# A DiT block on one core: batch 1's input from a second queue, one more matmul row before two scale groups, and a gate vector folded by copies

## The chip, the cores and the metric

The kernel runs on one NeuronCore of a Trainium2 chip. Its engines are TensorE (matrix multiplication), VectorE (elementwise work and reductions), ScalarE (activation functions, also elementwise), GpSimd and SyncE; the last issues most of the DMAs here. In the profile they are PE (with PEld for TensorE's weight loads), DVE, ACT, POOL and SP. The metric is the device time in microseconds of one execution; lower is better.

## What is computed

A transformer block with adaptive layer norm. Two batches of 256 tokens of width 1152, two heads of 576, and a hidden width of 4608, in bf16:

```python
B, N, D = (2, 256, 1152); F = 4 * D; H = 2
mod = (_silu(c) @ w_mod).reshape(B, 6, 1, D)
shift_a, scale_a, gate_a, shift_m, scale_m, gate_m = [mod[:, i] for i in range(6)]
h = _layernorm(x, axis=-1) * (1 + scale_a) + shift_a
qkv = (h @ wqkv).reshape(B, N, 3, H, Dh)
# ... softmax attention of q, k, v over each batch and head ...
x = x + gate_a * (a @ wo)
h2 = _layernorm(x, axis=-1) * (1 + scale_m) + shift_m
m = _gelu(h2 @ w_fc1) @ w_fc2
return x + gate_m * m
```

The six modulation vectors come from the small input c (two rows of 1152) and a matrix of 1152 x 6912. Two of them matter below: scale_a, which is needed at the very start, and gate_m, which is needed at the very end.

## The kernel before: the parts that are touched

The weights stream through a ring of large buffers, nearly all of them issued in order from SyncE's queue (`nc.sync`). The kernel begins with x, whose 512 rows are four tiles of 128 partitions. A partition of a batch holds two neighbouring rows of x, one in each of the batch's two tiles, so that tiles 0 and 1 are batch 0 and tiles 2 and 3 batch 1.

```python
    x_v = x.rearrange("b (p l) d -> p b l d", l=TPB)
# ...
    x_sb = act.tile([P, NT, D], BF16, name="x_sb", tag="x_sb")
    c_sb = act.tile([B * KD, P], BF16, name="c_sb")
    nc.scalar.dma_start(c_sb[:], c_v)
    touch_x = act.tile([P, 32], BF16, name="touch_x")
    nc.scalar.dma_start(touch_x[:], x_v[:, 1, 0, 0:32])
    for t in (0, 1, 3, 2):
        nc.sync.dma_start(x_sb[:, t, :], x_v[:, t // TPB, t % TPB, :])
```

After x come the scale weights in groups of columns, each followed by the rows of the K weights that it is used with:

```python
    SGROUPS = [(0, 2), (2, 4), (4, 6), (6, 8), (8, 9)]
    KM1 = 6
    w_scale_a = wide_tile("w_scale_a")
# ...
    def load_k(k0, k1, c0, c1):
        nc.sync.dma_start(w_k[:, k0:k1, c0:c1], wqkv_v[:, k0:k1, D + c0:D + c1])

    for k0, k1 in SGROUPS:
        nc.sync.dma_start(
            w_scale_a[:, :, k0 * P:k1 * P],
            wmod_v[:, :, S_SCALE_A * D + k0 * P:S_SCALE_A * D + k1 * P],
        )
        for a, z in [(0, 1), (1, 2)] if k0 == 0 else [(k0, k1)]:
            load_k(a, z, 0, KM1 * P)
    load_k(0, KD, KM1 * P, D)
```

A little later in program order ScalarE loads its function tables (`InstLoadActFuncSet`). The layer norm's statistics are split over two engines: ScalarE sums tiles 0 and 2 (`act_stats`), VectorE takes tiles 1 and 3 (`stats_piece`). The normalized tiles are transposed on TensorE, scaled by 1 + scale_a while they are copied out of PSUM (`modulate`, batch 0 on VectorE, batch 1 on ScalarE), and multiplied with the K weights. Instructions of one engine run in the order in which they stand here:

```python
    warm(7, pwarm)
    act_stats(0)
    for j in range(NPD):
        stats_piece(1, j)
    act_mean_eps(0)
    act_root(0)
    nc.scalar.activation(rstd1[:, 1:2], mv1[:, 1, 1:2], ACT.Ln, bias=eps_t[:], scale=1.0)
    root_exp(0, 2)
    act_stats(2)
    for j in range(NPD):
        stats_piece(3, j)
    pool_eps(3)
    pool_rsqrt(3, 4)
    norm1(1, 0, CUT)
    norm1(0, 0, CUT)
    pt_a = transpose_x([0, 1, 2, 3], BT[0])
    act_mean_eps(2)
    act_root(2)
    root_exp(2, 3)
    norm1(3, 0, CUT)
    pm0, pm1 = [scale_group(k, k + 1, acc_tile) for k in range(2)]
    nc.vector.tensor_scalar_mul(hT0[:, 0, 0:N], pt_a[:, 0, :], pm0[:, 0, 0:1])
    nc.vector.tensor_copy(scale_a[:, 0:1, :], pm0[:])
    scale_add(pm1, 1, 2)
    modulate(pt_a, 1, 1, 0, 0, "d")
    norm1(2, 0, N)
    norm1(2, N, CUT)
    pt_c = aux_tile([P, 4, N], "pt", BF16)
    transpose_x([0, 1, 2, 3], [3], pt_c, 1)
    fill(1)
    k_step(0, 0, N)
    k_step(1, 0, N, 0, 2)
    modulate(pt_c, 0, 0, 1, 0, "a", P, N)
    transpose_x([0, 1], [2], pt_c, 0)
    k_step(1, 0, N, 2)
# ...
    k_step(1, N, T)
    k_step(2, 0, N)
    k_step(2, N, T)
    for k in range(3, KD):
        split = 2 if k in (3, 5) else 0
        k_step(k, 0, T, 0, split)
        if k in (3, 5, 7):
            k1 = min(k + 3, KD)
            scale_add(scale_group(k + 1, k1), k + 1, k1)
        if k < KD - 1:
            both(transpose_x([k + 1], range(NT)), k + 1)
        k_step(k, 0, T, split)
    for m in range(KM1):
        k_evac(m)
```

`k_step(k, c0, c1, m0, m1)` adds the product of one chunk k of 128 inputs to output panels m0 to m1 - 1, in columns c0 to c1 (columns 0 to 255 are batch 0, 256 to 511 batch 1). `scale_group` computes 1 + scale_a for a few chunks by matmuls with two columns. `both` modulates a chunk for both batches.

At the end of the block the last gate, gate_m, is needed as a row of 1152 numbers for each batch, spread over all partitions. VectorE multiplies the gate weights by silu(c) and adds up over the nine chunks, which leaves a sum over 128 partitions to be done:

```python
    fold = const.tile([P, 32], FP32, name="fold")
    nc.vector.tensor_reduce(fold[:], ident[:].rearrange("p (q a) -> p a q", a=32), axis=AX.X, op=ALU.add)
    gates_dram = tc.dram_tile([2, B, D], BF16, name="gates_dram")

    def broadcast_gate(g):
        gate = act.tile([P, B, D], BF16, name="gate", tag="gate")
        for b in range(B):
            nc.gpsimd.dma_start(gate[:, b, :], gates_dram[g, b:b + 1, :].partition_broadcast(P))
        return gate
# ...
    def gate_vector(g, wg):
        part = act.tile([P, B, D], FP32, name="part", tag="x_sb")
        folded = small.tile([P, B, D // 32], FP32, name="folded", tag="folded", bufs=1)
        for k in range(KD):
            for b in range(B):
                if k == 0:
                    nc.vector.tensor_scalar_mul(part[:, b, :], wg[:, k, :], s32[:, k, b:b + 1])
                else:
                    nc.vector.scalar_tensor_tensor(
                        part[:, b, :], wg[:, k, :], s32[:, k, b:b + 1], part[:, b, :],
                        op0=ALU.mult, op1=ALU.add,
                    )
        for b in range(B):
            for c in range(0, D, PW):
                blocks = work.tile([P, PW // 32, 32], FP32, name="tmp", tag="tmp", bufs=3)
                nc.vector.transpose(blocks[:].rearrange("p j r -> p (j r)"), part[:, b, c:c + PW])
                nc.vector.tensor_reduce(
                    folded[:, b, c // 32:(c + PW) // 32], blocks[:], axis=AX.X, op=ALU.add
                )

        return lambda: gate_vector_finish(g, folded)

    def gate_vector_finish(g, folded):
        rows = D // 32
        pg = aux_tile([rows, B, 32], "pg")
        for b in range(B):
            nc.tensor.matmul(pg[:, b, :], folded[:, b, :], fold[:], start=True, stop=True)
        nat = work.tile([rows, B, 32], BF16, name="nat_v", tag="nat_v", bufs=1)
        nc.vector.tensor_copy(nat[:], pg[:])
        for b in range(B):
            nc.gpsimd.dma_start(gates_dram[g, b, :].rearrange("(j r) -> j r", r=32), nat[:, b, :])
        return broadcast_gate(g)
```

TensorE does this last sum, with `fold` (four stacked 32 x 32 identities) as the moving operand, just before the last panel of the first MLP matrix; the result goes to DRAM and comes back as a broadcast:

```python
    gate_m = None
    for m in range(MSPLIT, KF):
        pacc = acc_tile([P, T], "pacc")
        for k in range(KD):
            f1_mm(pacc[:], m, k, 0, T, k == 0)
        nc.scalar.activation(gT[:, m, :], pacc[:], ACT.Gelu_apprx_tanh)
        if m == 22:
            gate_m_finish = gate_vector(1, w_gate_m)
        if m == KF - 2:
            gate_m = gate_m_finish()
        if m == MSPLIT:
            load_f2(0)
        if m > MSPLIT and m % KD == KD - 1:
            load_f2(m // KD)
```

The last matrix multiplies the 36 chunks of the hidden layer, and each finished group of 384 columns is multiplied by gate_m on VectorE:

```python
        pacc = acc_tile([P, cw], "pacc")
        for kk in range(KF):
            j, r = divmod(n * KF + kk, 27)
            nc.tensor.matmul(
                pacc[:], gT[:, kk, t * P:(t + 1) * P],
                w_f2[j][:, r, c0 - n * PW:c0 - n * PW + cw],
                start=(kk == 0), stop=(kk == KF - 1),
            )
        tmp = work.tile([P, cw], FP32, name="tmp", tag="tmp", bufs=3)
        nc.vector.tensor_tensor(tmp[:], pacc[:], gate_m[:, b, c0:c0 + cw], op=ALU.mult)
        o_sb = work.tile([P, cw], BF16, name="o_sb", tag="o_sb", bufs=3)
        (nc.vector if last else nc.gpsimd).tensor_tensor(
            o_sb[:], tmp[:], x1[:, t, c0:c0 + cw], op=ALU.add
        )
        nc.sync.dma_start(out_v[:, b, t % TPB, c0:c0 + cw], o_sb[:])
```

Of the kernel before, what the change touches and what calls it, by code (L numbers as in the profile page):

```python
# [8 lines left out]
FP32 = mybir.dt.float32  # L9
BF16 = mybir.dt.bfloat16  # L10
ACT = mybir.ActivationFunctionType
ALU = mybir.AluOpType
AX = mybir.AxisListType
# [6 lines left out]
def kernel(  # L20
# [11 lines left out]
    nc = tc.nc  # L32
    B, N, D = x.shape
# [3 lines left out]
    P = 128  # L37
    T = B * N
    NT = T // P
    TPB = N // P  # L40
    KD = D // P
    KF = F // P
# [10 lines left out]
    const = ctx.enter_context(tc.tile_pool(name="const", bufs=1))  # L53
    act = ctx.enter_context(tc.tile_pool(name="act", bufs=1))
    wide = ctx.enter_context(tc.tile_pool(name="wide", bufs=5))
    work = ctx.enter_context(tc.tile_pool(name="work", bufs=2))
    small = ctx.enter_context(tc.tile_pool(name="small", bufs=4))
# [5 lines left out]
    def aux_tile(shape, name, dt=FP32):  # L63
        return psum.tile(shape, dt, name=name, tag="aux", bufs=2)


    x_v = x.rearrange("b (p l) d -> p b l d", l=TPB)
# [14 lines left out]
    x_sb = act.tile([P, NT, D], BF16, name="x_sb", tag="x_sb")  # L82
# [1 line left out]
    nc.scalar.dma_start(c_sb[:], c_v)  # L84
    touch_x = act.tile([P, 32], BF16, name="touch_x")
    nc.scalar.dma_start(touch_x[:], x_v[:, 1, 0, 0:32])
    for t in (0, 1, 3, 2):
        nc.sync.dma_start(x_sb[:, t, :], x_v[:, t // TPB, t % TPB, :])  # L88

    zeros = const.tile([P, T], BF16, name="zeros")  # L90
# [39 lines left out]
    for (j0, j1), rows in zip(SHG, QROWS):  # L130
# [25 lines left out]
        act_func_set_id=LN_EXP_TABLES, name=nc.get_next_instruction_name(),  # L156
        engine=mybir.EngineType.Activation,
    ))
    neg_half = const.tile([P, B], FP32, name="neg_half")
    nc.gpsimd.memset(neg_half[:], -0.5)  # L160
    early = small.tile([P, 1], FP32, name="early", tag="early", bufs=1)
# [116 lines left out]
    def k_step(k, c0=0, c1=T, m0=0, m1=KM1):  # L278
        for m in range(m0, m1):
            if k == 0 and c0 == 0:  # L280
                pk[m] = acc_tile([P, T], "pk")
            nc.tensor.matmul(  # L282
                pk[m][:, c0:c1], w_k[:, k, m * P:(m + 1) * P], hT0[:, k, c0:c1],
                start=(k == 0 and c0 == 0), stop=(k == KD - 1), skip_group_check=True,
            )
# [112 lines left out]
    k_step(2, 0, N)  # L398
    k_step(2, N, T)
    for k in range(3, KD):  # L400
        split = 2 if k in (3, 5) else 0
        k_step(k, 0, T, 0, split)
        if k in (3, 5, 7):
            k1 = min(k + 3, KD)
            scale_add(scale_group(k + 1, k1), k + 1, k1)
        if k < KD - 1:
            both(transpose_x([k + 1], range(NT)), k + 1)
        k_step(k, 0, T, split)
    for m in range(KM1):
        k_evac(m)  # L410

# [38 lines left out]

    s32 = const.tile([P, KD, B], FP32, name="s32")
    nc.vector.tensor_copy(s32[:], sT[:, :, 0:B])
    fold = const.tile([P, 32], FP32, name="fold")
    nc.vector.tensor_reduce(fold[:], ident[:].rearrange("p (q a) -> p a q", a=32), axis=AX.X, op=ALU.add)
    gates_dram = tc.dram_tile([2, B, D], BF16, name="gates_dram")

    def broadcast_gate(g):
# [7 lines left out]
# [17 lines that stand above are left out]
                    folded[:, b, c // 32:(c + PW) // 32], blocks[:], axis=AX.X, op=ALU.add  # L482
                )

        return lambda: gate_vector_finish(g, folded)

    def gate_vector_finish(g, folded):
        rows = D // 32
        pg = aux_tile([rows, B, 32], "pg")
        for b in range(B):  # L490
            nc.tensor.matmul(pg[:, b, :], folded[:, b, :], fold[:], start=True, stop=True)
        nat = work.tile([rows, B, 32], BF16, name="nat_v", tag="nat_v", bufs=1)
        nc.vector.tensor_copy(nat[:], pg[:])  # L493
        for b in range(B):
            nc.gpsimd.dma_start(gates_dram[g, b, :].rearrange("(j r) -> j r", r=32), nat[:, b, :])  # L495
        return broadcast_gate(g)

    def gate_natural(g, wg):
# [278 lines left out]
# [4 lines that stand above are left out]
            f1_mm(pacc[:], m, k, 0, T, k == 0)  # L781
        nc.scalar.activation(gT[:, m, :], pacc[:], ACT.Gelu_apprx_tanh)  # L782
        if m == 22:
            gate_m_finish = gate_vector(1, w_gate_m)
        if m == KF - 2:
            gate_m = gate_m_finish()
        if m == MSPLIT:
            load_f2(0)
        if m > MSPLIT and m % KD == KD - 1:
            load_f2(m // KD)  # L790
# [9 lines left out]
    for gi, (n, t, c0, cw) in enumerate(groups):  # L800
        b = t // TPB
# [59 lines left out]
```

## Time and profile before

| what | value |
|---|---|
| time, median of 3 runs | 243.47 us (242.92 to 243.62) |
| span of the profiled execution | 241.3 us |
| TensorE busy | 236.3 us |
| first transposes of x on TensorE | 8.64 us |
| first matmul of the last K panels (L311) | 25.41 us |
| first and last matmul of the first MLP matrix (L750) | 97.31 to 167.87 us |
| end of the last matrix's matmuls (L806) | 238.18 us |

In the profile a line such as `L750` is line 750 of the kernel. The chain that ended last is followed back from the last instruction, at each step to whatever released it. The waits say for which other instruction or DMA an engine stood still. The timeline lists instructions in order of time, with equal ones merged: start, busy time, engine, line, operation, result and inputs, and in brackets the idle time before them. Times are microseconds from the start of the span. The ends of matmuls are modelled, so a single matmul in the list is longer than the step from one to the next.

### The profile page before, as it was taken

Reading aid. Unit: us, or ns where it says so; the run is one execution under the profiler, and the core shown is the slowest. Engines: PE = TensorE matmul, PEld = TensorE weight load, DVE = VectorE, ACT = ScalarE, POOL = GpSimd, SP = SyncE. Lnnn points to the kernel's source line nnn. Section 1 sums busy time; section 2 is a strip of 40 time slices with the busy share of each in tenths; the row PEclk is TensorE's granted clock in tenths of the full one; section 3 lists DMA queues with packets and bytes.
Section 4 is the critical chain, followed back from the end, with each engine's and each line's share of the span. In section 5 each row is a group of like instructions: output and inputs, shape, how many; then the busy total and the mean of one; then the engine's idle time right before and its main releaser. Section 6 shows DMA issues by size and latency. Waiting matters only on the chain.

```text
span 241.3 us, 3993 instructions
## 1 busy us (share of the span) xinstructions
PE 236.3 (98%) x1698; PEld 144.6 (60%) x1698; DVE 91.6 (38%) x194; ACT 60.1 (25%) x122; POOL 28.3 (12%) x47
## 2 busy tenths in 40 slices
PE   8899999999999999999999999999999999999994
PEld 5675444466667566888844444444666656666674
DVE  4842442319325678930002999950000000000001
ACT  6732322307215032770423333222000000000000
POOL 2300000001400324100000000001121111111111
PEclk9999999999999999999999999999999999999999
DMA  6999999998599994739999999999300000000000
GB/s 196 324 317 311 376 367 391 389 393 249 99 315 397 387 311 81 196 62 364 390 392 392 339 326 284 285 326 275 98 16 16 20 16 16 19 18 18 26 25 16
DMA packets 48925, 53.30 MB, mean 221 GB/s; under 512 B 9731, under 2 KB 36619, under 8 KB 48907
## 3 DMA queue, kind: packets, MB, share of 16 engines
q1 hardware_dynamic: 41312, 50.14, 62.6%
q10 hardware_dynamic: 7083, 1.72, 4.9%
q0 software_dynamic: 512, 1.19, 2.2%
q8 instruction: 13, 0.21, 0.4%
q14 instruction: 5, 0.04, 0.1%
HBM read 50.15 MB, written 1.19 MB: 213 GB/s over the span
## 4 chain that ended last, share of the span: by engine, by line
PE 95%; DMA 2%; DVE 1%; SPq 0%; issue 0%; DVEq 0%
PE pacc L806 29%; PE pacc L750 29%; PE pacc L697 7%; PE pacc L603 7%; PE pq L525 7%; PE pk L282 5%; PE pk L311 2%; DMA x_sb<-in_x_dram 2%; PE pa L644 2%; PE ps_s L560 2%; PE pn L420 2%; PE pt L267 1%; PE pm L250 1%; DVE stats L195 1%; PE pg L502 0%; SPq L88 0%
## 5 line engine op out<-in xcount | busy, mean ns | idle before, releaser
L750 PE MATMUL pacc<-hT,w_f 128*128 128x256 bf16 (+1 forms) x432 | 70.5, 326 | 0.0
L806 PE MATMUL pacc<-w_f,gT 128*128 128x384 bf16 (+2 forms) x468 | 70.5, 314 | 0.0
L806 PEld LDWEIGHTS <-gT 128*128 128x128 bf16 x468 | 44.4, 98 | 26.2
L750 PEld LDWEIGHTS <-w_f 128*128 128x128 bf16 x432 | 42.2, 98 | 27.6
L812 DVE TENSOR_TENSOR tmp<-pacc,gate 128x384 f32<-128x384 f32 (+2 forms) x13 | 6.9, 527 | 65.6 <-PE pacc L806 57.3
L782 ACT ACTIVATE gT<-pacc 128x512 bf16<-128x512 f32 x24 | 14.3, 597 | 32.7 <-PE pacc L750 32.7
L473 DVE SCALAR_TENSOR_TENSOR part<-w_gate_m,s,part 128x1152 f32<-128x1152 bf16 x16 | 21.4, 1414 | 0.0
L814 POOL TENSOR_TENSOR o_sb<-tmp,x 128x384 bf16<-128x384 f32 (+1 forms) x12 | 11.6, 971 | 53.9 <-DVE tmp L812 53.9
L697 PE MATMUL pacc<-w_o,big 128*128 128x384 bf16 x108 | 17.9, 326 | 0.0
L525 PE MATMUL pq<-hT,w_q 128*128 128x512 bf16 x81 | 17.8, 379 | 0.0
L603 PE MATMUL pacc<-w_v,hT 128*128 128x384 bf16 x108 | 17.7, 326 | 0.0
L603 PEld LDWEIGHTS <-hT 128*128 128x128 bf16 x108 | 10.5, 98 | 7.1 <-issue 0.3
L697 PEld LDWEIGHTS <-big 128*128 128x128 bf16 x108 | 10.4, 98 | 7.2 <-issue 0.4
L525 PEld LDWEIGHTS <-w_q 128*128 128x128 bf16 x81 | 7.9, 98 | 9.4
L282 PE MATMUL pk<-big,w_k 128*128 128x256 bf16 (+1 forms) x72 | 13.2, 325 | 0.0
L703 POOL TENSOR_TENSOR x<-tmp,x_sb 128x384 f32<-128x384 f32 x8 | 7.3, 911 | 26.3 <-DVE tmp L702 26.3
L471 DVE TENSOR_SCALAR part<-w_gate_m,s 128x1152 f32<-128x1152 bf16 x2 | 1.6, 818 | 22.2 <-DMA w_gate_m<-in_w_mod_dram 22.2
L495 POOL DMA_DIRECT2D gates_dram<-nat_v x2 | 1.1, 534 | 67.7 <-DVE nat_v L493 67.7
L282 PEld LDWEIGHTS <-w_k 128*128 128x128 bf16 x72 | 6.8, 97 | 3.5 <-issue 0.2
L771 ACT ACTIVATE gT<-pacc 128x512 bf16<-128x512 f32 x12 | 6.5, 597 | 9.1 <-PE pacc L750 9.1
L516 POOL DMA_DIRECT2D gates_dram<-nat x4 | 2.4, 596 | 49.8 <-DVE nat L513 48.4
L175 PE MATMUL pwarm<-zeros 128*128 128x256 f32 x18 | 6.7, 540 | 1.2 <-DVE eps_t L95 1.2
(106 smaller groups left out, 164.4 us busy)
## 6 DMA issues: line engine op xcount, KB each, us to landing
w_f<-in_w_fc_dram SPq DMA_DIRECT2D x12, 864.0 KB, 14.2
w_f<-in_w_fc_dram SPq DMA_DIRECT2D x3, 1728.0 KB, 10.1
w_f<-in_w_fc_dram SPq DMA_DIRECT2D x2, 2592.0 KB, 17.2
w_gate_a<-in_w_mod_dram SPq DMA_DIRECT2D x3, 864.0 KB, 14.4
w_v<-in_wqkv_dram SPq DMA_DIRECT2D x3, 864.0 KB, 15.4
w_o<-in_wo_dram SPq DMA_DIRECT2D x3, 864.0 KB, 14.7
w_shift_m<-in_w_mod_dram SPq DMA_DIRECT2D x3, 864.0 KB, 9.5
w_scale_m<-in_w_mod_dram SPq DMA_DIRECT2D x3, 864.0 KB, 15.8
```

The lines of the kernel that those rows point to most:

```text
L175: nc.tensor.matmul(dst[:, 0:T // 2], zeros32[:, 0:P], zeros32, start=True, stop=True)
L282: nc.tensor.matmul(pk[m][:, c0:c1], w_k[:, k, m * P:(m + 1) * P], hT0[:, k, c0:c1], start=(k == 0 and c0 == 0), stop=(k == KD - 1), skip_g ...
L473: nc.vector.scalar_tensor_tensor(part[:, b, :], wg[:, k, :], s32[:, k, b:b + 1], part[:, b, :], op0=ALU.mult, op1=ALU.add,)
L525: nc.tensor.matmul(pq[m][:], w_q[:, k, m * P:(m + 1) * P], hT[:, k, :], start=(k == 0), stop=(k == KD - 1), skip_group_check=True,)
L603: nc.tensor.matmul(pacc[:], hT[:, k, t * P:(t + 1) * P], w_v[:, k, pnl * PW:(pnl + 1) * PW], start=(k == 0), stop=(k == KD - 1),)
L697: nc.tensor.matmul(pacc[:], aT[:, k, t * P:(t + 1) * P], w_o[:, k, c0:c1], start=(k == 0), stop=(k == KD - 1),)
L703: (nc.gpsimd if pool_add else nc.vector).tensor_tensor(x1[:, t, c0:c1], tmp[:], x_sb[:, t, c0:c1], op=ALU.add)
L750: nc.tensor.matmul(dst, w_f1[m // KD][:, k, ml * P:(ml + 1) * P], hT[:, k, c0:c1], start=start, stop=(k == KD - 1), **kw,)
L782: nc.scalar.activation(gT[:, m, :], pacc[:], ACT.Gelu_apprx_tanh)
L806: nc.tensor.matmul(pacc[:], gT[:, kk, t * P:(t + 1) * P], w_f2[j][:, r, c0 - n * PW:c0 - n * PW + cw], start=(kk == 0), stop=(kk == KF - 1),)
L812: nc.vector.tensor_tensor(tmp[:], pacc[:], gate_m[:, b, c0:c0 + cw], op=ALU.mult)
L814: (nc.vector if last else nc.gpsimd).tensor_tensor(o_sb[:], tmp[:], x1[:, t, c0:c0 + cw], op=ALU.add)
```

## The change

Three things are changed.

First, SyncE loads only batch 0's two tiles of x, and then goes on to the scale weights. Batch 1's x comes in one load of 128 partitions with two neighbouring rows each (4608 bytes in one piece instead of two of 2304), issued from ScalarE's queue behind the table load, so that it may travel beside the first scale group.

Second, for chunks k = 3 and 5 three panels of the K product, and not two, stand ahead of the next scale group, so that this group's weights may come later; and for k = 4 and 6 the product is done batch by batch.

Third, the last sum of gate_m leaves TensorE: four copies bring the four groups of 32 partitions side by side in 32 partitions, VectorE adds and transposes them, and two stores write them to DRAM. This frees TensorE from the fold, and the gate need no longer be finished in two steps.

```diff
--- before.py
+++ after.py
@@ -84,7 +84,7 @@
     nc.scalar.dma_start(c_sb[:], c_v)
     touch_x = act.tile([P, 32], BF16, name="touch_x")
     nc.scalar.dma_start(touch_x[:], x_v[:, 1, 0, 0:32])
-    for t in (0, 1, 3, 2):
+    for t in range(TPB):
         nc.sync.dma_start(x_sb[:, t, :], x_v[:, t // TPB, t % TPB, :])
 
     zeros = const.tile([P, T], BF16, name="zeros")
@@ -156,6 +156,7 @@
         act_func_set_id=LN_EXP_TABLES, name=nc.get_next_instruction_name(),
         engine=mybir.EngineType.Activation,
     ))
+    nc.scalar.dma_start(x_sb[:, TPB:NT, :], x_v[:, 1, :, :])
     neg_half = const.tile([P, B], FP32, name="neg_half")
     nc.gpsimd.memset(neg_half[:], -0.5)
     early = small.tile([P, 1], FP32, name="early", tag="early", bufs=1)
@@ -398,14 +399,15 @@
     k_step(2, 0, N)
     k_step(2, N, T)
     for k in range(3, KD):
-        split = 2 if k in (3, 5) else 0
+        split = 3 if k in (3, 5) else 0
         k_step(k, 0, T, 0, split)
         if k in (3, 5, 7):
             k1 = min(k + 3, KD)
             scale_add(scale_group(k + 1, k1), k + 1, k1)
         if k < KD - 1:
             both(transpose_x([k + 1], range(NT)), k + 1)
-        k_step(k, 0, T, split)
+        for c0, c1 in ((0, N), (N, T)) if k in (4, 6) else ((0, T),):
+            k_step(k, c0, c1, split)
     for m in range(KM1):
         k_evac(m)
 
@@ -450,8 +452,6 @@
 
     s32 = const.tile([P, KD, B], FP32, name="s32")
     nc.vector.tensor_copy(s32[:], sT[:, :, 0:B])
-    fold = const.tile([P, 32], FP32, name="fold")
-    nc.vector.tensor_reduce(fold[:], ident[:].rearrange("p (q a) -> p a q", a=32), axis=AX.X, op=ALU.add)
     gates_dram = tc.dram_tile([2, B, D], BF16, name="gates_dram")
 
     def broadcast_gate(g):
@@ -482,17 +482,24 @@
                     folded[:, b, c // 32:(c + PW) // 32], blocks[:], axis=AX.X, op=ALU.add
                 )
 
-        return lambda: gate_vector_finish(g, folded)
-
-    def gate_vector_finish(g, folded):
         rows = D // 32
-        pg = aux_tile([rows, B, 32], "pg")
-        for b in range(B):
-            nc.tensor.matmul(pg[:, b, :], folded[:, b, :], fold[:], start=True, stop=True)
-        nat = work.tile([rows, B, 32], BF16, name="nat_v", tag="nat_v", bufs=1)
-        nc.vector.tensor_copy(nat[:], pg[:])
-        for b in range(B):
-            nc.gpsimd.dma_start(gates_dram[g, b, :].rearrange("(j r) -> j r", r=32), nat[:, b, :])
+        quads = small.tile([32, P // 32, B * rows], FP32, name="quads", tag="quads", bufs=1)
+        for a in range(P // 32):
+            nc.gpsimd.dma_start(quads[:, a, :], folded[32 * a:32 * (a + 1), :, :].rearrange("p b j -> p (b j)"))
+        total = small.tile([32, 96], FP32, name="total", tag="total", bufs=1)
+        nc.vector.memset(total[:], 0.0)
+        nc.vector.tensor_reduce(
+            total[:, 0:B * rows], quads[:].rearrange("p a c -> p c a"), axis=AX.X, op=ALU.add,
+        )
+        turned = small.tile([32, 96], FP32, name="turned", tag="turned", bufs=1)
+        nc.vector.transpose(turned[:], total[:])
+        nat = small.tile([32, 96], BF16, name="nat_v", tag="nat_v", bufs=1)
+        nc.vector.tensor_copy(nat[:], turned[:])
+        flat = gates_dram[g, :, :].rearrange("b (j r) -> (b j) r", r=32)
+        nc.gpsimd.dma_start(
+            flat[0:64, :].rearrange("(q c) r -> c q r", q=2), nat[:, 0:64].rearrange("c (q r) -> c q r", q=2),
+        )
+        nc.gpsimd.dma_start(flat[64:B * rows, :], nat[0:B * rows - 64, 64:96])
         return broadcast_gate(g)
 
     def gate_natural(g, wg):
@@ -781,9 +788,7 @@
             f1_mm(pacc[:], m, k, 0, T, k == 0)
         nc.scalar.activation(gT[:, m, :], pacc[:], ACT.Gelu_apprx_tanh)
         if m == 22:
-            gate_m_finish = gate_vector(1, w_gate_m)
-        if m == KF - 2:
-            gate_m = gate_m_finish()
+            gate_m = gate_vector(1, w_gate_m)
         if m == MSPLIT:
             load_f2(0)
         if m > MSPLIT and m % KD == KD - 1:
```

## The prediction

> **What bounds the kernel now.** I read the page first: busy times, then the chain that ended last, then the chain in order of time for the first 33 us, then the timeline around each thing that the diff touches.
>
> ```profile
> span 241.3 us, 3993 instructions
> PE 236.3 (98%) x1698; PEld 144.6 (60%) x1698; DVE 91.6 (38%) x194; ACT 60.1 (25%) x122; POOL 28.3 (12%) x47
> ...
> PE 95%; DMA 2%; DVE 1%; SPq 0%; issue 0%; DVEq 0%
> ```
>
> TensorE is busy for 98% of the span and is 95% of the chain. So only three kinds of edit can matter: one that changes TensorE's own work, one that changes the 8.6 us before its first useful work, and one that removes a gap in its stream. The gaps stand in the answer to what the weight loads waited for in the first 34 us:
>
> ```profile
> PEld L267 <- DVE xn L235: 1.3, 2, 1.1
> ...
> PEld L250 <- DMA w_scale_a<-in_w_mod_dram: 0.7, 2, 0.5
> ...
> PEld L420 <- DMA w_shift_a<-in_w_mod_dram: 0.4, 1, 0.4
> ```
>
> The columns are us in total, times, longest. The middle line is what "later scale groups" aims at. These are idle times of the weight load, which normally hides behind the matmul before it, so the loss of the matmul stream is smaller. I get it from the chain's pieces: 18 undisturbed matmuls of 512 columns (L311) take 3.88 us, 0.216 us each; 8 of 256 columns take 0.90 us, 0.112 us each. Before the first of the two waits, 20 of 256 columns take 2.41 us instead of 20 x 0.112 = 2.25: 0.16 us lost. Before the second, 8 of 512 take 1.77 instead of 1.72: 0.05 us. The shift vectors (L420) take 0.74 us where the later ones take 0.62: 0.12 us. That makes **0.33 us** of loss through late weights.
>
> The start of the chain, and the timeline of the two engines that it runs through:
>
> ```profile
> 1.63 4.60 DMA x_sb<-in_x_dram
> 6.23 0.02 issue
> 6.25 1.49 DVE stats L195 x3
> 7.75 0.02 issue
> 7.77 0.04 DVE mv L197
> 7.80 0.12 issue
> 7.92 0.68 DVE xn L235 x2
> 8.60 0.04 issue
> 8.64 0.62 PE pt L267 x8
> ```
>
> ```profile
> 3.62 1.25 ACT L208 ACTIVATE sink<-x_sb 128x1152 f32<-128x1152 bf16 x1
> ...
> 4.42 1.48 DVE L195 BATCH_NORM_STATS2 stats<-x_sb 128x6 f32<-128x384 bf16 x3
> ```
>
> VectorE does tile 1's statistics from 4.42 us, when that tile lands, finishes its aggregate at about 6.18, and starts tile 3 at 6.25; tile 3 landed at 1.63 + 4.60 = 6.23. Only then, in program order, do the normalizations come (7.92) that the first transposes need. So two things set the start nearly together: tile 1's landing at 4.42 plus two statistics (2 x 1.48 + 0.24), and tile 3's landing at 6.23. Tile 2 lands last: the x loads took 2.9 to 5.1 us to landing, and 5.1 after the fourth issue (about 2.1) is 7.2. It costs nothing now, since ScalarE takes it up at 7.23, straight after its earlier work.
>
> **What the Trainium skill says.** (1) "DMA: Bandwidth & Descriptors", section "Issuing engines are not separate DMA queues": loads started by different engines run on the same 16 DMA engines and interleave; a second issuer saves only issue time. Its section "Queues, rings and completion order" adds that each DMA engine goes round-robin between the rows that have work. Nothing large runs on a second queue at the start of the kernel before, so its trace can't confirm the sharing; what it does show is that the DMA share is 1.02 to 1.06 from 2.5 to 5.0 us, so there is nothing to gain by sharing then, and 0.62 and 0.83 in the two half microseconds from 5.0 to 6.0. (2) "TensorE: Matmul & The Clock Gate", table at its head (it stands before the first section): ScalarE's instruction queue is 8 deep and strictly in order. I read that to mean that the issuing sequencer may run ahead of the engine. The trace agrees: a transposing DMA (L554) is issued at 59.56 us while a ScalarE copy that is earlier in program order starts at 59.87. (3) The same page, "Back-to-back issue gap": columns/2.4 + 2.5 ns, so 216 ns for 512 columns and 109 for 256. The trace has 216 and 112.
>
> **The change, part by part.**
>
> *The fold of gate_m by copies.* Removed from TensorE: four fp32 matmuls (L491) in the middle of the first MLP matrix. The chain gives them 165.57 to 165.82, **-0.26 us** of pure path. Also removed: one reduction (L454, 0.36 us of VectorE at 32.8 us), beside TensorE work that doesn't wait for it. Added: four copies from SBUF to SBUF, a memset, a reduction, a 32x32 transpose, a cast and two stores, none on TensorE. Do they make the gate late? `folded` is ready at 159.86 + 0.55 = 160.41. Four issues by GpSimd at 0.53 us each (L495: two in 1.06) end at 162.5; landing 2.1 to 3.7 us after the last issue (the two median landings of such small DMAs on the page) gives 164.1 to 165.7; some 0.8 us of VectorE (estimated from the 0.57 and 0.55 us of the larger transpose and reduction and the 0.22 us cast) gives 164.9 to 166.5. From there on it is as before: the stores issued at 166.37 led to the first use of the gate at 174.40, 8.0 us. So the gate is there at 173 to 175, against 174.40 before. The first group of the last matrix is done by 167.87 + 5.86 = 173.73, and with six accumulators TensorE waits only if the gate is some 5 x 5.86 = 29 us late. No cost.
>
> *Later scale groups.* For k = 3 and 5, three instead of two matmuls of 512 columns stand ahead of the scale group, so TensorE asks for its weights 0.216 us later. That covers the lost 0.16 and 0.05 us: **-0.21 us**. In exchange fewer matmuls (three, 0.65 us, not four, 0.86) lie between the next chunk's transpose and its use. VectorE then ScalarE modulate that chunk: 16.34 to 16.69 and 16.72 to 17.19. After the change TensorE would come to it at 16.28 + 0.65 + 0.22 = 17.15, too early for the batch 1 half by a hair, and that is what the split of k = 4 and 6 into column halves is for: batch 1's half is first read 6 x 0.112 = 0.67 us later. The split's own cost: 12 x 0.112 - 6 x 0.216 = 0.05 us each, **+0.10 us** for two.
>
> *Batch 1's x in one load from ScalarE.* The issue: ScalarE's queue issues the small c and x loads until 1.74 us, then the table load runs from 1.77 to 3.05. By point (2) the new issue should go out at about 1.8 us, while the table load runs; if not, at 3.1. From an issue to its first bytes takes about 0.9 us or more (issue at 0.73, first traffic after 1.5), so the 576 KB begin to flow at about 3.0. *What it does for batch 0:* adding the half-microsecond rates (87, 143, 383, 378 GB/s) gives 306 KB moved by 3.0 us: x tile 0 is through and tile 1 (295 KB) hardly begun. If the rings share one to one, tile 1 needs 0.8 us more than alone at full rate; if the new load comes late, nothing. I take **+0.4 us** on tile 1's landing, so 4.8. *What it does for batch 1:* all of x is 1.18 MB; from 306 KB at 3.0 us and at 350 GB/s it is moved by 5.5, and landing was about 0.6 us after the last byte for tile 0 (moved by 3.0, taken up at 3.62): about 6.1. Tile 3 thus lands as before and tile 2 a microsecond earlier, where ScalarE is busy until 7.2 anyway. Then VectorE's two statistics after tile 1 are the bound: normalization 0.4 us later. Of that, the stream of TensorE has slack at the transposes of tile 2 (0.20 us of idle at 11.08, set by ScalarE's chain, which doesn't move): **+0.2 us** net. *What it does for the weights:* the first scale group is issued at 1.63 instead of 2.57, and the dip from 5.0 to 6.0 is filled (about 0.37 of 16 engines for 1 us, or 0.13 MB, some 0.4 us earlier for all that follows). Together with a slightly later TensorE this removes the third loss too: **-0.1 us**.
>
> Sum: -0.26 - 0.21 + 0.10 + 0.2 - 0.1 = -0.27 us. From 243.47 that is **243.2 us**.
>
> **The rivals.** *A: the x load crowds out batch 0.* Its packets are twice as long, so in a round-robin by packets it may take two thirds of the bandwidth, tile 1 lands up to 1.2 us late, and all behind it shifts. For it: nothing in the old trace competes with tile 1, and VectorE's order puts both statistics ahead of the first normalization. Against it: a later TensorE also stops losing to late weights. It would make +0.8 more than my sum: 244.0. *B: the x load goes out behind the table load and beside the first scale group*, flows from 4.2 us, and lands at about 6.8: the statistics of tile 3 start 0.6 us later, and the net is about +0.4 - 0.57 + 0.10, 243.4. *C: the start doesn't move at all*, because ScalarE's chain and not VectorE's sets the dense part of the stream, or the load fits into the dip: -0.47, 243.0. *D: the gate by copies becomes the bound* of the last matrix; the slack of 29 us speaks against it, and it would not show in the time.
>
> **Range and chances.** All parts together lie between -0.6 (C with all losses gone) and +0.8 (A), and the three runs before spread over 0.7 us. A range of 242.4 to 244.1 should hold it 8 times in 10. 2% is 4.9 us; no part comes near it. Faster by over 2%: 0.01, within 2%: 0.975, slower by over 2%: 0.015.
>
> **What would show each step.** Right: L491 is gone and L750's stream runs through; the waits of L250 for w_scale_a are gone; the x issue of ScalarE stands at about 1.8 us and tile 1's statistics at about 4.8; the first transposes at about 9.0 instead of 8.64; the first k panel done (L311 begins, 25.41 before) within 0.3 us of before. Wrong: an issue at 3.1 (then B), tile 1's statistics after 5.4 (A) or at 4.4 (C), a new wait of k = 4 or 6 for ScalarE's modulation, or L806 waiting for the gate. The prediction fails as a whole if the first weights, pushed aside by x on a second ring, make TensorE wait for whole microseconds in the first 12 us.

## The result and the profile after

The changed kernel takes 246.66 us (median of 6 runs) against 243.69 us for the kernel before (median of 6): a ratio of 1.0131, 95% interval 1.011 to 1.0152. It is 3 us slower, and the predicted range of 242.4 to 244.1 us doesn't hold it.

The head of the page of the kernel after, its first rows:

```profile
span 245.0 us, 4005 instructions
PE 235.9 (96%) x1695; PEld 146.2 (60%) x1706; DVE 92.2 (38%) x196; ACT 60.2 (25%) x122; POOL 30.3 (12%) x51
PEclk9979999999999999999999999999999999999999
```

TensorE's busy time is what it was, the span is 3.7 us longer, and one digit of the clock row is not a 9. Both signs point to the start. The chain of the kernel after, in order of time:

```profile
1.80 7.40 DMA x_sb<-in_x_dram
9.20 0.02 issue
9.22 1.49 DVE stats L196 x3
10.71 0.02 issue
10.74 0.04 DVE mv L198
...
11.62 0.74 PE pt L268 x8
...
13.70 1.71 PE pk L283 x8
```

Batch 1's x, issued at 1.80, lands at 9.20 us. Before, its first tile landed at 6.23. VectorE takes up tile 3's statistics at 9.22 and not 6.25, and the first transposes come at 11.62 and not 8.64. Then there is a second loss: 8 matmuls of 256 columns take 1.71 us. The kernel before had:

```profile
10.26 0.90 PE pk L282 x8
```

The stretches of the kernel after show why (start and end, length, busy time and instructions of TensorE, its weight loads, VectorE, ScalarE and GpSimd, then granted clock, DMA share, GB/s):

```profile
10.00:11.00 1.00, 0.00 (x0) 0.00 (x0) 0.97 (x4) 0.97 (x3) 0.00 (x0) 1.00 1.16 315
...
12.00:13.00 1.00, 1.00 (x26) 0.79 (x24) 0.58 (x2) 0.50 (x2) 0.59 (x3) 0.50 1.18 309
13.00:14.00 1.00, 1.00 (x10) 0.81 (x8) 0.96 (x6) 0.37 (x1) 0.00 (x0) 0.50 1.17 309
```

TensorE has nothing to do from 7.5 to 11.6 us, as its line in the timeline says (in brackets the idle time before it):

```profile
11.62 0.74 PE L268 MATMUL pt<-ident,xn 128*128 128x128 bf16 x8 [4.12 <-DVE xn L236]
```

From 12.0 to 15.4 us its clock is granted at half. The Trainium skill, "TensorE: Matmul & The Clock Gate", Part 1 (The HAM clock gate), describes this: a free-running window of about 3.4 us in which TensorE is idle halves the clock, and a busy one restores it. The trace agrees on the length: 0.50 for 3.4 us. On what counts as idle it agrees less well. The clock falls 0.4 us after TensorE has taken up work, so that the 3.4 us before the fall (8.57 to 11.98) hold 0.36 us of work; and in the profiled execution of x_only (below) 3.06 us of idle time in one piece, 8.37 to 11.43, left the clock at 1.00.

The chains of the two profiled executions, cut at common points, give the whole account:

| from, to | before, us | after, us | difference |
|---|---|---|---|
| start to first transposes | 8.64 | 11.62 | +2.98 |
| to the four matmuls behind tile 2's transposes | 2.73 | 3.95 | +1.22 |
| to the first of the last K panels | 14.04 | 13.85 | -0.19 |
| to the first MLP matrix | 71.90 | 71.90 | 0 |
| to the last matrix | 70.56 | 70.20 | -0.36 |
| to the last matmul's end | 70.31 | 70.30 | -0.01 |

The sum is +3.64 us. The late x costs the first two rows, 4.2 us, and the fold brings back 0.36. The -0.19 can't be put down to the later scale groups alone: x_only, which leaves them as they were, takes 13.91 us for that stretch, because a TensorE that comes later finds its weights there.

### The profile page after: what moved, and what is told of

Read it like the earlier page. It is cut to its first block, busy times and chain, and to the rows that moved or that the text cites. A ratio compares the mean times of both kernels' runs of the same rounds, so it can differ in the third digit from the quotient of the medians.

```text
span 245.0 us, 4005 instructions
## 1 busy us (share of the span) xinstructions
PE 235.9 (96%) x1695; PEld 146.2 (60%) x1706; DVE 92.2 (38%) x196; ACT 60.2 (25%) x122; POOL 30.3 (12%) x51
## 4 chain that ended last, share of the span: by engine, by line
PE 94%; DMA 3%; DVE 1%; issue 0%; ACTq 0%; ACT 0%; DVEq 0%
PE pacc L811 29%; PE pacc L757 29%; PE pacc L704 7%; PE pacc L610 7%; PE pq L532 7%; PE pk L283 5%; DMA x_sb<-in_x_dram 3%; PE pk L312 2%; PE pa L651 2%; PE ps_s L567 2%; PE pn L422 1%; PE pt L268 1%; PE pm L251 1%; DVE stats L196 1%; PE pg L509 0%
## 5 line engine op out<-in xcount | busy, mean ns | idle before, releaser
L283 PE MATMUL pk<-big,w_k 128*128 128x256 bf16 (+1 forms) x82 | 13.8, 316 | 0.1
L283 PEld LDWEIGHTS <-w_k 128*128 128x128 bf16 x84 | 8.4, 103 | 2.8 <-issue 0.2
L488 POOL DMA_DIRECT2D quads<-folded x4 | 2.0, 508 | 61.9 <-DVE total L490 61.9
L709 DVE TENSOR_TENSOR tmp<-pacc,gate 128x384 f32<-128x384 f32 x12 | 6.6, 549 | 3.1 <-PE pacc L704 3.1
```

Source lines behind the costliest of these rows:

```text
L283: nc.tensor.matmul(pk[m][:, c0:c1], w_k[:, k, m * P:(m + 1) * P], hT0[:, k, c0:c1], start=(k == 0 and c0 == 0), stop=(k == KD - 1), skip_g ...
L709: nc.vector.tensor_tensor(tmp[:], pacc[:], gate_a[:, b, c0:c1], op=ALU.mult)
```

## The experiments

**Which part does it.** x_back gives the changed kernel its old x loads back:

```diff
-    for t in range(TPB):
+    for t in (0, 1, 3, 2):
         nc.sync.dma_start(x_sb[:, t, :], x_v[:, t // TPB, t % TPB, :])
     ...
-    nc.scalar.dma_start(x_sb[:, TPB:NT, :], x_v[:, 1, :, :])
```

> The changed kernel with batch 1's x loaded as before: two loads of single rows from SyncE's queue, tile 3 then tile 2, ahead of the first scale group. The other two parts of the change stay. Theory (the whole loss comes from the x load, the other parts gain a little): first transposes at 8.6 us, no 0.50 clock after 11.5 us, time 0.2 to 0.6 us under the kernel before, about 243.2. Rival (the halves of k = 4 and 6, or the fold by copies, cost something themselves): time at or above the kernel before.

242.98 us against 243.31, ratio 0.9981 (0.9971 to 0.9991). The theory holds: all of the loss is in the x load, and the other two parts gain a third of a microsecond. x_only is the counterpart, the kernel before with nothing but the x load changed:

```diff
-    for t in (0, 1, 3, 2):
+    for t in range(TPB):
     ...
+    nc.scalar.dma_start(x_sb[:, TPB:NT, :], x_v[:, 1, :, :])
```

> The kernel before with only the first part of the change: batch 0's x from SyncE, batch 1's in one load of double rows from ScalarE's queue. Theory (the loss is the x load's, and the other two parts gain 0.3 to 0.4 us whatever stands beside them): 246.9 to 247.3, landing at 9.0 to 9.6. Rival (the earlier scale groups or the halves of k = 4 and 6 add to the loss): 246.3 or less.

Four runs, 245.65 to 249.33 us, median 248.07, ratio 1.0203 (1.0161 to 1.0245). The median meets neither expectation, but the runs sort by granted clock: 1.0 in the one of 245.65, 0.991 in that of 247.3, 0.986 in the two of 248.8 and 249.3. In the profiled one (245.65) x lands at 9.01, as expected, and the first transposes come at 11.43, as in the changed kernel. So the wait for x is there without the other parts. By estimate, 3.4 us at 0.50 lower the mean clock of 245 us by 0.007, so that the other runs would have lost one or two such stretches; only the execution without one was profiled. fold_only and groups_only are the kernel before with the third and the second part alone. fold_only, against the kernel before (shortened; the new lines are those of the change):

```diff
-        pg = aux_tile([rows, B, 32], "pg")
-        for b in range(B):
-            nc.tensor.matmul(pg[:, b, :], folded[:, b, :], fold[:], start=True, stop=True)
+        for a in range(P // 32):
+            nc.gpsimd.dma_start(quads[:, a, :], folded[32 * a:32 * (a + 1), :, :].rearrange("p b j -> p (b j)"))
+        ...
```

> The kernel before with only the third part of the change: gate_m folded by copies. Theory (four fp32 matmuls leave TensorE's path, the gate comes in time): 0.25 to 0.4 us faster than before, ratio 0.9983 to 0.9990. Rival (the gain of x_back, 0.33 us, comes from the scale groups): no difference from before.

242.93 against 243.39, ratio 0.9985 (0.9973 to 0.9997): the fold gains what was expected of it.

groups_only:

```diff
-        split = 2 if k in (3, 5) else 0
+        split = 3 if k in (3, 5) else 0
     ...
-        k_step(k, 0, T, split)
+        for c0, c1 in ((0, N), (N, T)) if k in (4, 6) else ((0, T),):
+            k_step(k, c0, c1, split)
```

> The kernel before with only the second part of the change: three panels ahead of the scale groups after k = 3 and 5, and k = 4 and 6 batch by batch. Theory of the prediction: 0.21 us of waits gained, 0.10 lost by the shorter matmuls, so 0.1 us faster, ratio 0.9996. Rival (it carries the gain of x_back): 0.3 us faster, 0.9987. Other rival (the waits only move): 0.1 us slower.

243.26 against 243.39, ratio 0.9993 (0.9981 to 1.0004). The difference has the expected size, and can't be told from none.

**The clock.** warm_more keeps TensorE busy for longer before the first transposes:

```diff
-    warm(7, pwarm)
+    warm(13, pwarm)
```

> The changed kernel with 13 instead of 7 warming matmuls before the first transposes, so that TensorE is busy while it waits for batch 1's x. Theory (of the 4.0 us lost at the start, 3.0 are the wait for x and the rest is TensorE's clock, at 0.50 from 12 to 15 us): the clock stays at 1.00, the 8 matmuls of 256 columns that took 1.71 us take 0.9, and 1.0 to 1.3 us come back: 245.4 to 245.7. Rival (the slow matmuls from 12 to 15 us come from late operands, not from the clock): the time stays at 246.7.

Four runs, three of them 245.41 to 245.78 (the fourth, at a clock of 0.993, 247.35); median 245.61, ratio 1.0107 (1.0071 to 1.0143). The same stretches in its profile:

```profile
12.00:13.00 1.00, 1.00 (x24) 0.88 (x24) 0.41 (x1) 0.68 (x4) 0.95 (x3) 1.00 1.17 308
13.00:14.00 1.00, 1.00 (x20) 0.90 (x17) 0.92 (x5) 0.50 (x2) 0.00 (x0) 1.00 1.17 315
```

The clock is 1.00, and 20 instead of 10 matmuls fit into the microsecond from 13 to 14. From the first transposes to the first MLP matrix it takes 100.35 - 11.98 = 88.37 us, the changed kernel 101.32 - 11.62 = 89.70. So the clock accounts for 1.3 us of the profiled execution (1.05 between the medians of the two kernels), and the rest of the loss is the wait. The profiled execution of x_only, at a clock of 1.00, confirms it: from the first transposes to the four matmuls behind tile 2's it takes 2.62 us, where the changed kernel takes 3.95.

**Why x lands at 9.2 us.** no_touch leaves out a small load, touch_x, that stands in ScalarE's queue ahead of x and whose data nothing uses:

```diff
-    nc.scalar.dma_start(touch_x[:], x_v[:, 1, 0, 0:32])
```

> The changed kernel without the small load touch_x (128 pieces of 64 bytes, used by nothing), which stands in ScalarE's queue ahead of batch 1's x. Theory 1 (batch 1's x waits in its own ring behind the 128 small pieces, which each wait for a turn beside SyncE's loads): its bytes begin to move at about 3 us instead of 4.7, and it lands at 6.0 to 7.0 us instead of 9.2; tile 1 may land later, 4.5 to 5.3; first transposes at 8.7 to 9.5 instead of 11.6; time 243.3 to 244.5. Theory 2 (it shares the DMA engines with the first scale group and the K rows, whatever starts first): landing 8.5 us or later, time 246 or more.

243.81 us against 243.31, ratio 1.0015 (0.9999 to 1.0032). x begins before 4 us and lands at 7.5, the first transposes come at 9.89: theory 1, though with a later landing than it gave. touch_behind leaves nothing out and only exchanges two issues on ScalarE:

```diff
-    nc.scalar.dma_start(touch_x[:], x_v[:, 1, 0, 0:32])
     ...
     nc.scalar.dma_start(x_sb[:, TPB:NT, :], x_v[:, 1, :, :])
+    nc.scalar.dma_start(touch_x[:], x_v[:, 1, 0, 0:32])
```

> The changed kernel with touch_x issued behind batch 1's x in ScalarE's queue instead of ahead of it; nothing is left out. Theory (the place in the ring): as without touch_x, x begins before 4 us and lands at 7.0 to 7.6 us, time 243.5 to 244.3. Rival (the small pieces take turns from all loads wherever they stand): landing at 8.5 us or later, time 246 or more.

243.17 us against 243.55, ratio 1.0006 (0.9984 to 1.0029): the 3 us are back by this exchange alone. (4 of its 20 runs, at a clock of 0.992 or 0.993, take 245.3 to 245.6; a gain over the kernel before isn't shown.) From the timeline of touch_behind, in the fastest of its runs:

```profile
1.41 0.36 ACTq L158 DMA_DIRECT2D x_sb<-in_x_dram  x1
1.80 0.44 ACTq L159 DMA_DIRECT2D touch_x<-in_x_dram  x1
...
6.23 1.48 DVE L196 BATCH_NORM_STATS2 stats<-x_sb 128x6 f32<-128x384 bf16 x3
...
8.62 0.62 PE L268 MATMUL pt<-ident,xn 128*128 128x128 bf16 x8
```

The landing (6.2) is earlier than expected and 3 us earlier than in the changed kernel. So it is the small load ahead of x that costs them. But the exchange does two things: x no longer stands behind touch_x in its ring, and it is issued 0.4 us earlier, at 1.41 and not 1.80, which is ahead of SyncE's issue of the first scale group (1.63) and not behind it. touch_twice puts a second such load ahead of x:

```diff
     nc.scalar.dma_start(touch_x[:], x_v[:, 1, 0, 0:32])
+    touch_y = act.tile([P, 32], BF16, name="touch_y")
+    nc.scalar.dma_start(touch_y[:], x_v[:, 1, 0, 32:64])
```

> The changed kernel with a second small load like touch_x (128 pieces of 64 bytes) ahead of batch 1's x in ScalarE's queue. Theory (x waits in its ring for the small pieces, 8 on each DMA engine and each a turn beside SyncE's loads): x begins 1 to 1.8 us later than in the changed kernel (bulk after 6 us instead of 4.7) and lands at 10 to 11 us. Rival (turns only): landing within 0.4 us of 9.2.

Half met: the bulk begins another microsecond later, as the theory says, but lands at 9.27, where the rival had it. What each ring moved shows how the wait comes about. q10 is ScalarE's ring, q1 SyncE's; the lines give packets (in the profile about one for each piece of a load), MB and share of the DMA engines. The changed kernel from 4 to 5 us, then from 5 to 6, then from 7 to 8:

```profile
q1 hardware_dynamic: 543, 0.28, 99.3%
q10 hardware_dynamic: 62, 0.02, 8.4%
```

```profile
q10 hardware_dynamic: 47, 0.22, 84.4%
q1 hardware_dynamic: 176, 0.09, 34.3%
```

```profile
q1 hardware_dynamic: 276, 0.22, 72.9%
q10 hardware_dynamic: 31, 0.12, 30.3%
```

And no_touch from 4 to 5 us:

```profile
q10 hardware_dynamic: 84, 0.38, 97.6%
q1 hardware_dynamic: 7, 0.01, 1.7%
```

The Trainium skill, "DMA: Bandwidth & Descriptors", section "Queues, rings and completion order", says that a DMA engine goes round the rings that have work, drains a whole packet from one ring before it switches (there a packet is 9 to 17 pieces typically, at most 64, and not one piece as in the profile), and consumes each ring in its own order. The traces agree on the order and on long turns. They don't show what the expectations above took for granted, that every small piece waits for a turn of its own. Taken by quarter microseconds, the changed kernel moves nearly all of touch_x (141 packets) from 3.75 to 4.25 us, when SyncE's ring is nearly through with tile 1. From 4.25 to 4.75 ScalarE's ring moves nothing, and SyncE's moves 286 packets of the first scale group at 97%. x begins after 4.75, has the better of it for a while, and its last packets come one by one between the K weights'. In no_touch it is the other way round: x moves alone from 4.25 to 4.75 (45 packets, and none of SyncE's ring), and the scale group comes after it. two_rows (below) shows the same wait without small pieces: behind tile 3's 288 KB SyncE's ring has 4.5 to 5.5 us almost to itself (517 packets against 29), and most of tile 2 moves after that. So it isn't the time of the small pieces themselves that holds x back, which is half a microsecond, but the bulk of the other ring that goes ahead of x after them.

Two accounts say why it goes ahead, and no run here separates them: the turn of the other ring that follows each load, or the order of issue over both rings. x in no_touch and touch_behind and tile 3 in two_rows were issued (1.41 to 1.42 us) before the first scale group (1.63 or 1.64) and went ahead of it; x in the changed kernel (1.80) and tile 2 in two_rows (1.8) were issued after it and went behind. A strict order of issue it isn't: when x began, at 4.75, at most 497 packets of the group's 1152 pieces had moved.

The MB of ScalarE's ring in all the kernels of this question:

| kernel | 3-4 us | 4-5 | 5-6 | 6-7 | 7-8 | 8-9 | landing, us |
|---|---|---|---|---|---|---|---|
| changed kernel | 0.01 | 0.02 | 0.22 | 0.20 | 0.12 | 0.03 | 9.2 |
| touch_twice | 0.01 | 0.00 | 0.02 | 0.22 | 0.30 | 0.06 | 9.3 |
| no_touch | 0.10 | 0.38 | 0.07 | 0.04 | 0.00 | 0.00 | 7.5 |
| touch_behind | 0.10 | 0.41 | 0.08 | 0.00 | 0.00 | 0.00 | 6.2 |
| hold_weights | 0.06 | 0.24 | 0.27 | 0.03 | 0.00 | 0.00 | 6.8 |
| hold_no_touch | 0.09 | 0.38 | 0.10 | 0.02 | 0.00 | 0.00 | 7.1 |

The last two belong to the question of sharing: SyncE issues the first scale group only when batch 1's x has landed, with touch_x in place and without it. Their times (244.92 and 245.64 us) contain that delay of the weights and are not to be compared.

```diff
+    scale_loads = []
     ...
-        nc.sync.dma_start(
+        scale_loads.append(nc.sync.dma_start(
     ...
-    nc.scalar.dma_start(x_sb[:, TPB:NT, :], x_v[:, 1, :, :])
+    x_late = nc.scalar.dma_start(x_sb[:, TPB:NT, :], x_v[:, 1, :, :])
+    tc.add_manual_dep(scale_loads[0], x_late.ins.name, WAIT_FOR, reason="x first")
```

> The changed kernel, touch_x in place, but the first scale group (and all of SyncE's queue behind it) is only issued when batch 1's x has landed. Its total time isn't to be read, only the landing. Theory 1 and 2 together (x starts late behind touch_x, and from there on shares the DMA engines with the first weights): x starts as late as touch_x allows, but without large loads beside it touch_x itself ends sooner; landing at 5.5 to 6.8 us instead of 9.2. Theory 1 alone (only its own ring holds it back): landing at 8.5 us or later, as in the changed kernel.

> hold_weights without touch_x: batch 1's x neither stands behind the small pieces nor shares the DMA engines with the first weights (which are issued only when it has landed). Only the landing is to be read. Theory (two causes, the late start behind touch_x and the sharing with the weights, make up the late landing; either alone costs less than both): landing at 5.8 to 6.5 us, against 6.8 with touch_x alone, 7.5 with the weights alone and 9.2 with both. Rival (a load of long rows from ScalarE's queue has a slow tail of its own): 6.8 us or later here too.

With touch_x and no weights beside it x lands at 6.8, as expected. The small pieces are through only a quarter of a microsecond sooner there (most of them move from 3.5 to 4.0 us), but x follows at once. Without either x still lands at 7.1, not at 5.8 to 6.5, where the rival of that run had it. That is one execution, and touch_behind landed the same load at 6.2 with the weights beside it, so 7 us is no lower bound. The two conditions don't add. touch_x costs 1.7 to 3 us (9.2 against 7.5 and 6.2) **because** the first weights of the other ring go ahead of x when it stands there; either of the two alone costs little or nothing.

**One load or two.** sp_double lets SyncE issue the same double-row load, right behind tile 1:

```diff
     for t in range(TPB):
         nc.sync.dma_start(x_sb[:, t, :], x_v[:, t // TPB, t % TPB, :])
+    nc.sync.dma_start(x_sb[:, TPB:NT, :], x_v[:, 1, :, :])
     ...
-    nc.scalar.dma_start(x_sb[:, TPB:NT, :], x_v[:, 1, :, :])
```

> The changed kernel with batch 1's x still in one load of double rows, but issued by SyncE right behind tile 1 and ahead of the first scale group. Theory 1 (the ring behind touch_x) and theory 2 (sharing with the weights) both expect that it lands at 6.0 to 7.2 us, since nothing of its own ring and no weights stand before it; time 243 to 243.8. Rival (the long rows, or one semaphore for both tiles, are slow in themselves): landing at 8 us or later, time 245 or more.

It lands at 6.92, the first transposes come at 9.33, and the time is 244.37 us, ratio 1.0051 (1.0034 to 1.0068), outside the expected 243.8. x_back, with the same bytes at the same place in two loads, had its transposes at 8.37. That one load makes tile 3, which VectorE needs first, wait for tile 2 as well, explains little of this: VectorE waits 0.21 us for the double load. Most of it is that tile 1's statistics start at 4.96 and not at 4.31 us; why tile 1 lands later ahead of the double load stays open, and the profile is of the fastest of the 20 runs. Besides, 6 of the 20 runs of sp_double, at a clock of 0.992 or 0.993, take 245.6 to 245.9. two_rows cuts the load in ScalarE's queue in two (without touch_x, tile 3 first):

```diff
-    nc.scalar.dma_start(x_sb[:, TPB:NT, :], x_v[:, 1, :, :])
+    for t in (3, 2):
+        nc.scalar.dma_start(x_sb[:, t, :], x_v[:, 1, t % TPB, :])
```

> no_touch with batch 1's x in two loads of single rows from ScalarE's queue, tile 3 first, as SyncE had them. Theory (in one load, tile 3, which VectorE needs first, can't be used before tile 2 has landed too): tile 3 lands at 6.0 to 6.5 us instead of 7.5, first transposes at 8.5 to 9.1, time 242.9 to 243.3. Rival (the sharing with tile 1 and the weights sets the landing, however it is cut): tile 3 lands after 7.2, time 243.7 or more.

243.92 us, ratio 1.0023 (1.0009 to 1.0037), tile 3 at 6.97 and tile 2 at 8.1. That is no better than no_touch. The time is where the rival had it and the landing of tile 3 between the two: from this queue the cut gains half a microsecond for tile 3 and loses as much for tile 2.

**Where the wait passes on.** In order_swap VectorE normalizes tiles 1 and 0 before it takes tile 3's statistics:

```diff
+    norm1(1, 0, CUT)
+    norm1(0, 0, CUT)
     for j in range(NPD):
         stats_piece(3, j)
     pool_eps(3)
     pool_rsqrt(3, 4)
-    norm1(1, 0, CUT)
-    norm1(0, 0, CUT)
```

> The changed kernel, with VectorE's normalization of tiles 1 and 0 moved ahead of its statistics of tile 3. Nothing else moves. Theory (batch 0's transposes wait for batch 1's x only through VectorE's program order): first transposes at 8.0 us instead of 11.6, though x lands at 9.2 as before; the stream then stops at tile 3's transposes until about 12.3, so of the 4 us lost 1 to 2 come back: 244.7 to 245.7. Rival (the late x holds TensorE by something else): first transposes stay at 11 us or later.

x lands at 9.09, and the first transposes come at 8.64 all the same (not quite at 8.0), so it is VectorE's order that hands the wait to batch 0. The time is less clear: two runs at 244.97 and 244.99 us (clock 1.0 and 0.999), two at 247.2 and 248.0 (clock 0.993 and 0.986); median 246.08, ratio 1.0108 (1.0048 to 1.0168). TensorE's idle time is cut in pieces, not removed. back_swap tries the same order with the old x loads and without touch_x, and back_no_touch is its pair without the swap:

> x_back (batch 1's x as before, the other two parts of the change kept) without touch_x. Theory (touch_x's small pieces take turns from SyncE's loads, 8 to 10% of the DMA share from 3 to 4 us): x lands 0.1 to 0.3 us earlier, time 242.7 to 242.9. Rival (touch_x opens the way to batch 1's half of x, the reason why it is there): x lands later, time 243 to 243.5.

> back_no_touch (the fold by copies and the later scale groups, batch 1's x from SyncE in single rows, no touch_x) with the same swap on VectorE. Theory (VectorE's two statistics set the start): first transposes 0.3 to 0.5 us earlier, but tile 3's transposes up to 0.7 us later, so little changes: 242.6 to 243.1. Rival (the start is the whole bound): 242.4 to 242.6.

back_no_touch takes 242.94 us, ratio 0.9977 (0.9967 to 0.9986). It can't be told from x_back. In its profile tile 1's statistics start later than there (4.71 against 4.31), not earlier, but in the time touch_x in its old place is neither a help nor a burden. The swap makes it worse, 243.89, ratio 1.0036 (1.002 to 1.0052), where 242.6 to 243.1 us was expected: batch 0's transposes come at 8.0 instead of 8.8, tile 3's at 11.05 instead of 9.9. And its 20 runs fall into two groups, 12 of 243.7 to 243.9 us at a clock of 0.999 or 1.0, and 8 of 245.0 to 246.0 at 0.993. **The version that beats both kernels** is then the change without its first part, with touch_x (x_back, 0.9981) or without it (back_no_touch, 0.9977).

## Why the prediction was wrong, point by point

- **The step that failed is "What it does for batch 1".** It let all of x move at 350 GB/s from 3.0 us on, "moved by 5.5", landing at "about 6.1". It landed at 9.2. The issue time was right (1.80 us, during the table load, as the queue depth suggested), but I took an issue for a start: I had named the small x load as what comes before it, and did not ask what goes ahead of x when something stands ahead of it in its ring. What went ahead was the first scale group (286 packets of it from 4.25 to 4.75 us, and none of x). The prediction had feared the opposite, weights pushed aside by x. touch_behind shows that the small load ahead of x is worth the 3 us; whether through its place in the ring or through the later issue of x stays open.
- **The clock was not in the sum at all.** The page before has 9 in all 40 slices, so I never asked what an idle TensorE costs after the wait. It cost 1.2 us in the chain and 1.3 us against warm_more.
- **Tile 1's landing, "+0.4 us":** its statistics start at 4.50 against 4.42, so +0.08. Rival A, in which x crowds out batch 0, is wrong; it was the weights that crowded out x. Rival B had a late x too, but by an issue at 3.1 us that didn't happen, and with 0.6 us of delay instead of 3.0.
- **The weights, -0.1 and -0.21:** the waits for the scale weights are gone from the changed kernel, as forecast. It is a poor gain, because TensorE comes 3 us later, and they are gone from x_only too, which has the old groups. In x_back, which starts at 8.37 and not 8.64, a wait of the weight load for the scale weights of 0.6 us is back in spite of the third panel, and the last K panels begin at 25.32 against 25.41: of the 0.27 us that the start gains two thirds are given back there.
- **The split, +0.10:** 12 matmuls of 256 columns take 1.31 us (k = 6 in the changed kernel), 0.109 each, against 6 x 0.216 = 1.29. The cost is 0.02 us each, not 0.05, because 0.112 was too long.
- **The fold, -0.26 and no cost:** right, and a little small. The first MLP matrix is 0.36 us shorter. The gate came late in one step and early in another. From the timeline of the kernel after:

```profile
164.53 2.01 POOL L488 DMA_DIRECT2D quads<-folded  x4 [61.86 <-DVE total L490]
...
171.61 0.63 DVE L491 TENSOR_REDUCE total<-quads 32x72 f32<-32x288 f32 x1 [7.27 <-DMA quads<-folded]
...
178.86 0.56 DVE L817 TENSOR_TENSOR tmp<-pacc,gate 128x384 f32<-128x384 f32 x1 [6.09 <-DMA gate<-gates_dram]
```

The four copies landed 5.1 us after the last was issued, where I had 2.1 to 3.7; the stores and the broadcast then took 5.8 us from the first store's issue at 173.06, where I had 8.0. The first group of the last matrix is done at about 177.4 and waits 1.5 us for the gate in its accumulator, which TensorE doesn't notice: its last stretch is 70.30 us, as before.

Three figures of the working are off without bearing on the outcome. The 306 KB by 3.0 us are the sum of the first three rates; the fourth, 378 GB/s, belongs to 3.0 to 3.5. The dip in the DMA share from 5.0 to 6.0 us is some 0.3 of the engines for 1 us, not 0.37. And rival A's +0.8 is counted from the predicted 243.2, so that it is +0.5 from the kernel before.

What stays open is why the double-row load takes until about 7 us even without touch_x and weights (hold_no_touch). Most of it is moved by 6.0, and a few packets (0.02 MB) follow later. The profile doesn't say on which of the 16 DMA engines they are. Landings of such loads also differ between runs: no_touch and touch_behind issued x at the same time, ahead of everything but c in its ring, and landed it at 7.5 and 6.2.

## What to carry to other kernels

A load that others wait for goes to the head of its ring and is issued before the bulk loads of the other rings. In these traces one ring had the DMA engines almost to itself for half a microsecond or more, and with 8 KB ahead of x the other ring's bulk went first. An issue time read from a trace is not yet a start: ask what else has been issued by then. A microsecond of waiting at the start of a TensorE-bound kernel can cost more than itself, so estimate with the idle stretch what the clock does after it. Whether a load is better cut in two is to be tried in its place: from SyncE's queue two loads took 242.98 us and one 244.37, from ScalarE's the cut gained nothing (243.92 against 243.81).

## What the runs showed of the hardware

- With a load of 128 pieces of 64 bytes, 8 KB in all, ahead of it in its ring, the bulk of a 576 KB load moved from 4.75 to 8.5 us and not from 3.5 to 5.5, while another ring had bulk to move. Nearly all of the small load itself moved from 3.75 to 4.25 us.
- Two rings with bulk did not share the DMA engines evenly from piece to piece: from 4.25 to 4.75 us the changed kernel moved 286 packets of SyncE's ring and none of ScalarE's, no_touch none of SyncE's and 45 of ScalarE's.
- A DMA issue of ScalarE went out at 1.80 us while its table load ran from 1.77 to 3.05.
- After 4.1 us without work TensorE's clock was 0.50 for 3.4 us (12.0 to 15.4), beginning 0.4 us after the work did. After 3.06 us without work it stayed at 1.00 in the profiled execution of x_only. In that of back_swap it fell to 0.50 from 11.5 to 14.9 us, after idle stretches of 0.73, 0.47 and 1.25 us. By their mean clock, 8 of the 20 runs of back_swap and 6 of sp_double had such a stretch, at 1.3 to 1.5 us each.
- Four copies of 9 KB between partitions of SBUF, issued by GpSimd beside the loads of the last weights, landed 5.1 us after the last issue.
